# Copying the first pair's high rows by VectorE in a fused attention and MLP kernel

## The chip, the cores and the metric

The kernel runs on one core of a Trainium2 chip. A core has a matrix engine (TensorE, PE in the profile), a vector engine (VectorE, DVE), an activation engine (ScalarE, ACT), GpSimd (POOL) and a queue engine (SyncE, SP) that here only issues DMAs. The metric is the device time of one execution in microseconds (us), the median of three runs.

## The reference, cut to what matters

There are 4 batches, 8 heads, 576 tokens and a head width of 64. Attention with a decay comes first, then a gated MLP that also mixes tokens, then a second MLP with a gate. All of it is wanted in float32 accuracy.

```python
scores = scale * np.matmul(q, k.transpose(0, 1, 3, 2))
log_f = np.log(np.clip(f, 0.0001, 1.0))
cum = np.cumsum(log_f, axis=-1)
decay = cum[:, :, :, None] - cum[:, :, None, :]
scores = np.where(causal, -1000000000.0, scores + decay)
attn = softmax(scores)                     # written out in the reference
x = np.matmul(attn, v)                     # heads side by side: 512 wide
h = np.maximum(x @ w_in, 0.0)              # 512 -> 1024, halves u and v
v_n = (v - mean) / np.sqrt(var + 1e-06)
v_s = np.einsum('ts,bsd->btd', w_spatial, v_n) + b_spatial[None, :, None]
x = (u * v_s) @ w_out
xk = mu_k * x + (1.0 - mu_k) * x_prev      # the same with mu_r for xr
out = sigmoid(xr @ w_r) * (np.maximum(xk @ w_k, 0.0) ** 2 @ w_v)
```

## The kernel before

**Pairs of heads.** The 32 heads (batch by batch) are worked on as 16 pairs, numbered 0 to 15. For each pair q and k are loaded (`load`, L214), scaled by a power of two, and split into a high part in float16 (`qkhi`: `nq` by DVE on L258, `nk` by ACT on L256 for pair 0 and by POOL on L254 for the others) and the rest (`qklo`, L266 on DVE). Both parts lie side by side in `nk` and `nq`, and a DMA transpose (L268) turns them into the stacks `kT` and `qT` with 128 rows: 64 of one part, 64 of the other.

**The second stack.** A score is high times high plus the two cross products. `kT` times `qT` gives the cross products. The product of the high parts, with the decay, comes from a second pair of stacks: `kA` holds the 64 high rows of k and three rows of decay, `qA` the 64 high rows of q and three rows of a constant. The high rows are in `kT` and `qT` already and are copied from there: `kaux` (L274) copies rows 0 to 63 of `kT` to `kA`, `qaux` (L280) copies rows 64 to 127 of `qT` to rows 0 to 63 of `qA`. A copy is 64 rows of 1280 float16 values. L275 fetches the decay rows from DRAM (`cumd`). All four transfers are DMAs of the SP queue. The stacks exist three times: pair p uses stack p modulo 3.

**Scores, twice.** First the scores are made with queries as rows (`score`, L298: one matmul of `kT` and `qT`, then one of `kA` and `qA` into the same bank), DVE takes the row maxima from them (`rowmax`, L309), POOL scales these (L318), and ACT sums the exponentials (`rowsum`, L321). `mrow` puts maximum and logarithm of the sum into one row per query, turns it over by a matmul (L337), copies it (`mr`, L339 on DVE), and three small DMAs (L341) write it into three more rows of `qA`. Then the scores are made again with keys as rows (`scoreT`, L352), exponentiated (L362), cut to the causal part (L366 on POOL) and multiplied with v (L393).

**The MLPs.** The first MLP of a batch (L530 and L528, L598, L615) runs on PE between the attention of later pairs. The second MLP (L927) follows after the last pair. Weights arrive as 64-bit values and are converted by ACT and DVE (L103, L106, L110, L111).

**What sets the order.** Each step of each pair has a due time from the table `P` (two units for each pair), `run` emits the steps in order of due time, and a scheduler with its own model of time then fixes one order for each engine's instructions and for the DMAs of each queue. Steps under `high_priority(PRIO)` are preferred by it. `vl2` is the due time of the loads of v for batch 2 (L217). Every engine, and the SP queue, works strictly in its order: a DMA whose source isn't ready holds all DMAs behind it.

Of the kernel before, what the change touches and what calls it, by code (L numbers as in the profile page):

```python
# [25 lines left out]
T3 = ((0, 0), (0, 1), (1, 0))  # L26
# [3 lines left out]
SU = (((4, 0, 512, 0),), ((3, 0, 448, 0), (4, 512, 64, 448)), ((2, 0, 320, 0), (1, 0, 192, 320)), ((0, 0, 64, 0),))  # L30


P = dict(load=-8.0, sq=-5.52, ss=-5.2, sc=-5.0, hik=-5.196, lok=-4.166, hiq=-4.2, loq=-3.95, aux=-3.539, s=-2.53, m=-0.78, t=0.0, tu=0.426, th=0.412, pv0=0.2, pv1=0.9, out=1.405, rc=1.219, nr=1.831, xs=0.977, xl=1.55, rs=0.06, w1=-3.8, w0=2.0, s1=1.5, s0=6.8, wd=0.6, sd=0.6, wsp=9.493, eb=13.318, ed=1.1, crow=-4.2, mlp0=2.7, mlp1=2.7, mlp2=3.608, mlp3=2.7, len0=6.684, len1=6.952, len2=6.757, len3=4.319, T1=0.0, T2=0.0, T3=0.02, T4=0.0, T5=0.0, T6=0.0, T7=0.044, L1=0.0, L2=-0.017, L3=0.0, L4=0.0, L5=-0.224, L6=-0.408, L7=0.04, v0=-3.174, vs0=0.15, T8=0.0, T9=0.0, T10=0.0, T11=0.0, T12=-0.061, T13=-0.031, T14=0.069, T15=0.0, L0=0.0, L8=0.0, L9=0.0, L10=0.0, L11=0.0, L12=0.0, L13=-0.003, L14=0.0, L15=-0.24, vl1=-5.062, vq1=-2.7, vl2=-4.971, vq2=-2.898, vl3=-3.679, vq3=-3.376, lv0=0.238, lu0=0.381, lg0=0.249, lv1=0.238, lu1=0.381, lg1=0.199, lv2=0.238, lu2=0.381, lg2=0.436, lv3=0.346, lu3=0.381, lg3=0.701, n1=0.385, n2=0.508, n3=1.019, n4=1.161, gs=0.05, ta=3.45, tb=1.65, tc=0.22, fnb=1, fnk=1, fvn=1, fwf=0, fwin=0, fwsp=0)

PRIO = 300


def f32(ap):  # L40
# [3 lines left out]
class K:  # L44
# [201 lines left out]
    def qkhi(self, p, nm, eng):  # L246
# [5 lines left out]
        if eng == "act":  # L252
            if P["fnk"] > 0.5 and p >= 1:
                self.nc.gpsimd.tensor_scalar(hi, src, s, None, op0=ALU.mult)  # L254
# [15 lines left out]
    def kaux(self, p):  # L270

        nc = self.nc
        t = self.T["kA", p % 3]
        nc.sync.dma_start(t[0:64, 0:10], self.T["kT", p % 3][0:64, 0:10])  # L274
        nc.sync.dma_start(t[64:67, 0:10].rearrange("p (h c) t -> p h (c t)", h=2)[:, :, 64:640], self.cumd[:, 2 * p:2 * p + 2])  # L275

    def qaux(self, p):

        nc = self.nc
        nc.sync.dma_start(self.T["qA", p % 3][0:64], self.T["qT", p % 3][64:128])  # L280

    def crow(self, p):

# [28 lines left out]
    def rowsum(self, g, blocks):  # L312
# [4 lines left out]
        nb = self.at.tile([128, 10], F32, tag="nb", bufs=4, name="nb")  # L317
        (self.nc.gpsimd if P["fnb"] > 0.5 else self.nc.vector).tensor_scalar(nb[:, c], self.nm[p % 2][:, c], qa[:, 5:6], -1.0, op0=ALU.mult, op1=ALU.mult)  # L318
        for ib in blocks:
# [54 lines left out]
    def products(self, p, part):  # L374

        self.last = None
        with self.tc.high_priority(PRIO):
            if part == 0:
# [48 lines left out]
    def wconv(self, i):  # L427
# [3 lines left out]
        wf = self.wf[i] = self.stp.tile([128, 512], F32, tag="wf", bufs=4, name="wf")  # L431
        self.raw_convert(self.wst[i], wf, True, P["fwf"] > 0.5)
        self.sumsq(self.am[:, kc:kc + 1], wf, self.win[:, 0, kc, cs])
# [6 lines left out]
    def wsplit(self, i):  # L440
# [4 lines left out]
        hi, lo = self.win[:, 0, kc, cs], self.win[:, 1, kc, cs]  # L445
        self.pin(nc.gpsimd.tensor_scalar(hi, wf, s, None, op0=ALU.mult) if P["fwin"] > 0.5 else nc.scalar.mul(hi, wf, s))
        nc.vector.scalar_tensor_tensor(lo, wf, s, hi, ALU.mult, ALU.subtract)

    def weights_spatial(self):
# [300 lines left out]
    def early_norms(self):  # L750
# [127 lines left out]
    def m3(self, i):  # L878
# [265 lines left out]
```

## Time and profile before

| | |
|---|---|
| median of 3 runs | 689.62 us (688.99 to 691.65) |
| the profiled execution | 684.6 us, span of the core's work 682.9 us |
| PE busy | 616.9 us (90%) |
| DVE busy | 436.3 us (64%) |
| ACT busy | 462.7 us (68%) |
| POOL busy | 186.5 us (27%) |
| DMA | 69.74 MB |

A line of the profile gives the busy time of an engine or a group of instructions. Shares are averages over stages: attention with the first MLP takes about the first 350 us, the second MLP from about 420 us on is PE alone. [...]

### The profile page before, as it was taken

Reading aid. Unit: us, or ns where it says so; the run is one execution under the profiler, and the core shown is the slowest. Engines: PE = TensorE matmul, PEld = TensorE weight load, DVE = VectorE, ACT = ScalarE, POOL = GpSimd, SP = SyncE. Lnnn points to the kernel's source line nnn. Section 1 sums busy time; section 2 is a strip of 40 time slices with the busy share of each in tenths; the row PEclk is TensorE's granted clock in tenths of the full one; section 3 lists DMA queues with packets and bytes.
Section 4 is the critical chain, followed back from the end, with each engine's and each line's share of the span. In section 5 each row is a group of like instructions: output and inputs, shape, how many; then the busy total and the mean of one; then the engine's idle time right before and its main releaser. Section 6 shows DMA issues by size and latency. Waiting matters only on the chain.

```text
span 682.9 us, 11117 instructions
## 1 busy us (share of the span) xinstructions
PE 616.9 (90%) x3720; PEld 369.7 (54%) x3720; DVE 436.3 (64%) x1238; ACT 462.7 (68%) x1023; POOL 186.5 (27%) x420
## 2 busy tenths in 40 slices
PE   0478676998999999989999899999999999999997
PEld 0133333566545666446657544566655556566585
DVE  6885957879487867676137888997228524532342
ACT  4689899898879879788339599974328334442531
POOL 6342444674447743465106010000000000000000
PEclk9998898999999999999999999999999999999999
DMA  7984542627654555341046672313001100100010
GB/s 254 266 229 94 139 116 52 207 57 196 167 129 108 94 172 132 74 91 33 19 154 212 206 253 70 123 62 108 15 1 32 62 1 0 62 1 0 1 62 31
DMA packets 69343, 69.74 MB, mean 102 GB/s; under 512 B 46659, under 2 KB 47395, under 8 KB 69286
## 3 DMA queue, kind: packets, MB, share of 16 engines
q1 hardware_dynamic: 68854, 67.85, 35.5%
q10 hardware_dynamic: 432, 1.18, 0.4%
q8 instruction: 29, 0.48, 0.3%
q14 instruction: 28, 0.23, 0.1%
HBM read 43.61 MB, written 9.55 MB: 78 GB/s over the span
## 4 chain that ended last, share of the span: by engine, by line
PE 59%; DVE 14%; DMA 10%; ACT 7%; SPq 3%; issue 3%; POOL 2%; DVEq 0%; ACTq 0%
PE m L927 37%; PE o L393 4%; PE t L352 4%; DVE sx L309 4%; PE m L615 4%; PE s L298 3%; PE m1u L598 3%; DMA qA<-qT 3%; PE m1v L530 3%; SPq L341 2%; DMA qT<-nq 2%; ACT junk L70 2%; DMA wst<-in_moe_w_r_dram 2%; ACT junka L321 1%; DMA kT<-nk 1%
## 5 line engine op out<-in xcount | busy, mean ns | idle before, releaser
L321 ACT ACTIVATE junka<-sx,nb,qa 128x576 bf16<-128x576 f32 (+4 forms) x160 | 103.8, 648 | 20.5 <-POOL nb L318 17.3
L927 PE MATMUL m<-moe_w_v,k 128*128 128x512 f32 x432 | 111.6, 406 | 0.0
L927 PE MATMUL m<-xx,moe_w_k 128*128 128x512 f16 (+1 forms) x480 | 99.1, 358 | 0.6 <-ACT tmp L976 0.6
L927 PEld LDWEIGHTS m<-moe_w_v,k 128*128 128x128 f32 x432 | 80.7, 188 | 19.4
L309 DVE CUSTOM_DVE_ANT_0 sx<-s,mask 128x512 f32<-128x512 f32 (+4 forms) x160 | 72.5, 473 | 21.5 <-PE s L298 17.6
L298 PE MATMUL s<-kT,qT 128*128 128x512 f16 (+2 forms) x192 | 55.3, 308 | 25.3 <-DVE nm L309 14.2
L362 ACT ACTIVATE e<-t,qa 128x512 f32<-128x512 f32 x96 | 64.1, 680 | 18.5 <-PE t L352 18.0
L366 POOL TENSOR_SCALAR_AFFINE_SELECT e<-e 128x128 f32<-128x128 f32 x128 | 48.1, 388 | 85.2 <-ACT e L362 82.5
L927 PEld LDWEIGHTS <-moe_w_k 128*128 128x128 f16 x480 | 45.5, 98 | 47.6 <-issue 5.3
L976 ACT ACTIVATE tmp<-m,sx 128x512 f32<-128x512 f32 (+1 forms) x40 | 25.9, 647 | 58.6 <-PE m L927 58.6
L977 DVE TENSOR_TENSOR tmp<-tmp 128x512 f32<-128x512 f32 (+1 forms) x40 | 25.5, 638 | 56.9 <-ACT tmp L976 56.9
L393 PE MATMUL o<-e,v 128*64 128x64 f32 (+4 forms) x384 | 55.0, 410 | 5.2 <-DVE mr L339 1.9
L298 PE MATMUL s<-kA,qA 67*128 67x512 f16 (+2 forms) x192 | 49.0, 307 | 9.1 <-DMA qA<-qT 5.8
L899 POOL COPY x<-x 128x1 f32<-128x1 f32 x16 | 4.8, 313 | 185.5 <-ACT x L897 175.7
L615 PE MATMUL m<-wspT,vn 128*128 128x288 f16 x384 | 55.2, 286 | 0.2
L927 PE MATMUL m<-gh,moe_w_out 128*128 128x512 f16 (+1 forms) x240 | 50.9, 367 | 3.3 <-DVE gs L803 3.3
L352 PE MATMUL t<-qA,kA 70*128 70x512 f16 (+2 forms) x192 | 48.9, 292 | 3.9 <-DMA qA<-mr 2.9
L598 PE MATMUL m1u<-xt,win 128*128 128x288 f16 x384 | 52.3, 287 | 0.0
L352 PE MATMUL t<-qT,kT 128*128 128x512 f16 (+2 forms) x192 | 50.8, 292 | 0.0
L530 PE MATMUL m1v<-win,xt 128*128 128x512 f16 x192 | 49.4, 392 | 0.6 <-ACT xt L396 0.6
L927 PE MATMUL m<-moe_w_r,xx 128*128 128x512 f16 x216 | 48.0, 379 | 0.0
L949 DVE SCALAR_TENSOR_TENSOR mt<-x,mu,mt 128x64 f32<-128x64 f32 (+4 forms) x64 | 30.2, 514 | 26.7 <-ACT mt L947 26.7
(219 smaller groups left out, 1134.7 us busy)
## 6 DMA issues: line engine op xcount, KB each, us to landing
knat<-in_k_dram SPq DMA_DIRECT2D x16, 320.0 KB
v<-in_v_dram SPq DMA_DIRECT2D x20, 256.0 KB
gd<-u SPq DMA_DIRECT2D x16, 288.0 KB
gl<-gd SPq DMA_DIRECT2D x8, 576.0 KB
out_dram<-o SPq DMA_DIRECT2D x18, 256.0 KB
qnat<-in_q_dram SPq DMA_DIRECT2D x14, 320.0 KB
wst<-in_moe_w_k_dram SPq DMA_DIRECT2D x8, 512.0 KB
g<-gd SPq DMA_DIRECT2D x16, 256.0 KB
```

The costliest lines, as they stand in the source:

```text
L298: self.nc.tensor.matmul(s[:, o:o + n], self.tok(qn, p, h, 128 * ib - 64, 128)[0:r], self.tok(kn, p, h, k0, n)[0:r], start=(j == 0), stop=( ...
L309: self.nc.vector.tensor_tensor_reduce(out=self.sx[g][r0:, SO[ib] + k0:SO[ib] + k0 + n], in0=self.s[u % 2][r0:, o:o + n], in1=self.mask[r0: ...
L321: self.nc.scalar.activation(self.junka[r, 0:n], self.sx[g][r, SO[ib]:SO[ib] + n], AF.Exp, scale=qa[r, 5:6], bias=nb[r, i:i + 1], accum_out ...
L352: self.nc.tensor.matmul(t[:, o:o + n], self.tok(kn, p, h, 128 * c, 128)[0:r], self.tok(qn, p, h, q0, n)[0:r], start=(j == 0), stop=(j == 1))
L362: self.nc.scalar.activation(self.e[g][:, 512 * u:512 * u + 512], t, AF.Exp, scale=self.qa[p][:, 5:6])
L366: self.nc.gpsimd.affine_select(out=e, in_=e, pattern=[[1, 128]], compare_op=ALU.is_ge, fill=0.0, base=0, channel_multiplier=-1)
L393: self.chain(self.nc.tensor.matmul(o[r, 448 + f:448 + q1], v[:, c, pr, r], e, start=(c == 0), stop=(c == 4 or q1 == 64)))
L530: nc.tensor.matmul(self.m1p, xt[:, xs, 128 * j:128 * j + 128], self.win[:, ws, kc, 512:1024], **flags)
L598: self.nc.tensor.matmul(o, self.win[:, ws, kc, fs], self.xt[(4 * b + kc) % 8][:, xs, ts_], start=(kc == 0 and n == 0), stop=(kc == 3 and n ...
L615: nc.tensor.matmul(o, pairs[n][0], pairs[n][1], start=(n == 0), stop=(n == 13))
L927: self.nc.tensor.matmul(out, l, r, start=(first and j == 0), stop=(last and j == len(pairs) - 1))
L949: nc.vector.scalar_tensor_tensor(tmp[:, r0:r1], x2[:, kc, r0:r1], self.mu[:, w, 1, kc:kc + 1], tmp[:, r0:r1], ALU.mult, ALU.add)
```

## The change

For pairs below `NC`, which is 1, thus for pair 0 alone, the two copies of high rows are made by VectorE under the scheduler's preference. All other pairs keep their DMAs. In the table `P` one number differs: `vl2` is -3.989 where it was -4.971, so the five loads of v for batch 2 are due about half a pair's time later.

```diff
-P = dict(... vl2=-4.971, ...)
+P = dict(... vl2=-3.989, ...)
...
+NC = 1
...
         t = self.T["kA", p % 3]
-        nc.sync.dma_start(t[0:64, 0:10], self.T["kT", p % 3][0:64, 0:10])
+        if p < NC:
+            with self.tc.high_priority(PRIO):
+                nc.vector.tensor_copy(t[0:64, 0:10], self.T["kT", p % 3][0:64, 0:10])
+        else:
+            nc.sync.dma_start(t[0:64, 0:10], self.T["kT", p % 3][0:64, 0:10])
         nc.sync.dma_start(t[64:67, 0:10].rearrange("p (h c) t -> p h (c t)", h=2)[:, :, 64:640], self.cumd[:, 2 * p:2 * p + 2])
...
-        nc.sync.dma_start(self.T["qA", p % 3][0:64], self.T["qT", p % 3][64:128])
+        if p < NC:
+            with self.tc.high_priority(PRIO):
+                nc.vector.tensor_copy(self.T["qA", p % 3][0:64], self.T["qT", p % 3][64:128])
+        else:
+            nc.sync.dma_start(self.T["qA", p % 3][0:64], self.T["qT", p % 3][64:128])
```

Lines behind the edits have other numbers in the changed kernel (L268 is L269 there, L274 is L279, L275 is L280, L280 is L289, L341 is L350, L309 is L318). The scheduler gives new orders on all engines, from the first pair to the end. Three places matter below. In the names, kT_127, kA_128, qT_129 and qA_130 are the stacks of pairs 0, 3, 6 and so on, 131 to 134 those of pairs 1, 4, 7, and 135 to 138 those of pairs 2, 5, 8.

**VectorE at the start**, before: `qnat_89` and `knat_86` are pair 1's q and k, the L309 rows are pair 0's first row maxima.

```order
L258 TENSOR_SCALAR nq<-qnat_89,qa 128x10x64
L266 SCALAR_TENSOR_TENSOR nq<-qnat_89,qa,nq 128x10x64
L110 SCALAR_TENSOR_TENSOR wf<-wf,wst 128x512
L111 SCALAR_TENSOR_TENSOR wf<-wst,wf 128x512
L266 SCALAR_TENSOR_TENSOR nk<-knat_86,qa,nk 128x10x64
L309 ISA sx,nm_159<-s,mask 128x512
```

and in the changed kernel:

```order
L287 COPY qA_130<-qT_129 64x1280
L259 TENSOR_SCALAR nq<-qnat_89,qa 128x10x64
L267 SCALAR_TENSOR_TENSOR nq<-qnat_89,qa,nq 128x10x64
L111 SCALAR_TENSOR_TENSOR wf<-wf,wst 128x512
L277 COPY kA_128<-kT_127 64x1280
L112 SCALAR_TENSOR_TENSOR wf<-wst,wf 128x512
L318 ISA sx,nm_159<-s,mask 128x512
L318 ISA nm_159 128x1
L267 SCALAR_TENSOR_TENSOR nk<-knat_86,qa,nk 128x10x64
```

Both copies stand in front of the first row maximum, and pair 1's `nk` has moved behind it.

**The SP queue at the start**, from pair 0's decay rows to pair 1's last copy, before:

```order
L275 DMA kA_128<-cumd 3x2x576
L280 DMA qA_130<-qT_129 64x1280
L274 DMA kA_128<-kT_127 64x1280
L96 DMA wst<-in_moe_w_in_dram 128x1024
L217 DMA v_139<-in_v_dram 128x512 x5
L268 DMA_TRANSPOSE kT_131<-nk 128x10x128
L214 DMA knat_85<-in_k_dram 128x640
L268 DMA_TRANSPOSE qT_133<-nq 128x10x128
L214 DMA qnat_88<-in_q_dram 128x640
L274 DMA kA_132<-kT_131 64x1280
L275 DMA kA_132<-cumd 3x2x576
L280 DMA qA_134<-qT_133 64x1280
```

and in the changed kernel:

```order
L280 DMA kA_128<-cumd 3x2x576
L97 DMA wst<-in_moe_w_in_dram 128x1024
L218 DMA v_139<-in_v_dram 128x512 x5
L215 DMA knat_85<-in_k_dram 128x640
L269 DMA_TRANSPOSE qT_133<-nq 128x10x128
L269 DMA_TRANSPOSE kT_131<-nk 128x10x128
L215 DMA qnat_88<-in_q_dram 128x640
L280 DMA kA_132<-cumd 3x2x576
L289 DMA qA_134<-qT_133 64x1280
L279 DMA kA_132<-kT_131 64x1280
```

The two copies are gone from it, the loads behind them move up, and pair 1's q is transposed ahead of its k.

**The SP queue where `mr` rows and transposes meet.** Pair 5 (stacks 135 to 138), with the rows of pair 3 (qA_130<-mr), before:

```order
L275 DMA kA_136<-cumd 3x2x576
L268 DMA_TRANSPOSE qT_137<-nq 128x10x128
L341 DMA qA_130<-mr 1x10x128 x3
L268 DMA_TRANSPOSE kT_135<-nk 128x10x128
L280 DMA qA_138<-qT_137 64x1280
L214 DMA knat_87<-in_k_dram 128x640
L274 DMA kA_136<-kT_135 64x1280
```

and in the changed kernel:

```order
L280 DMA kA_136<-cumd 3x2x576
L269 DMA_TRANSPOSE qT_137<-nq 128x10x128
L269 DMA_TRANSPOSE kT_135<-nk 128x10x128
L350 DMA qA_130<-mr 1x10x128 x3
L279 DMA kA_136<-kT_135 64x1280
L289 DMA qA_138<-qT_137 64x1280
```

Pair 5's k is transposed ahead of pair 3's rows, no longer behind them.

Pair 7 (stacks 131 to 134) and pair 8 (135 to 138), with the rows of pair 5 (qA_138<-mr) and pair 6 (qA_130<-mr), before:

```order
L268 DMA_TRANSPOSE kT_131<-nk 128x10x128
L341 DMA qA_138<-mr 1x10x128 x3
L268 DMA_TRANSPOSE qT_133<-nq 128x10x128
L274 DMA kA_132<-kT_131 64x1280
L280 DMA qA_134<-qT_133 64x1280
...
L268 DMA_TRANSPOSE qT_137<-nq 128x10x128
L268 DMA_TRANSPOSE kT_135<-nk 128x10x128
L275 DMA kA_136<-cumd 3x2x576
L280 DMA qA_138<-qT_137 64x1280
L274 DMA kA_136<-kT_135 64x1280
...
L341 DMA qA_130<-mr 1x10x128 x3
```

and in the changed kernel:

```order
L350 DMA qA_138<-mr 1x10x128 x3
L280 DMA kA_132<-cumd 3x2x576
L269 DMA_TRANSPOSE kT_131<-nk 128x10x128
L269 DMA_TRANSPOSE qT_133<-nq 128x10x128
...
L269 DMA_TRANSPOSE qT_137<-nq 128x10x128
L218 DMA v_139<-in_v_dram 128x512
L215 DMA qnat_90<-in_q_dram 128x640
L289 DMA qA_138<-qT_137 64x1280
L218 DMA v_139<-in_v_dram 128x512
L350 DMA qA_130<-mr 1x10x128 x3
L269 DMA_TRANSPOSE kT_135<-nk 128x10x128
```

Here it is the other way round: pair 7's k and q both come behind pair 5's rows, and pair 8's k, which was ahead of pair 6's rows, comes behind them. Pair 11 has pair 7's exchange too: k, rows of pair 9, q before; rows of pair 9, k, q in the changed kernel. On PE, 10 matmuls of the first MLP's last product (L615) stand ahead of pair 8's first scores before, and 49 in the changed kernel. On ACT the squares of pair 2's q (L70) move one instruction ahead, in front of a weight's squares.

## Rows read from the trace of the kernel before

**Rows 1.** Busy time by stretches of 20 us; columns: engines, granted clock, DMA share, GB/s.
```profile
20.00:40.00 20.00, 10.73 (x43) 5.27 (x44) 16.73 (x57) 13.42 (x35) 7.34 (x10) 1.00 1.01 291
60.00:80.00 20.00, 13.44 (x69) 6.10 (x68) 15.59 (x47) 16.11 (x38) 8.42 (x14) 0.76 0.82 185
100.00:120.00 20.00, 14.53 (x91) 7.36 (x89) 15.26 (x57) 18.80 (x45) 8.63 (x18) 0.86 0.34 76
440.00:682.90 242.90, 239.03 (x1154) 146.27 (x1152) 115.12 (x238) 106.42 (x179) 1.47 (x8) 1.00 0.09 33
```

**Rows 2.** Chain of work that ended last; columns: start us, us, what.
```profile
25.49 4.55 DMA qT<-nq
30.06 4.23 DMA qA<-qT
...
98.01 3.48 DMA kT<-nk
101.50 2.68 DMA kA<-kT
```

**Rows 3.** Timeline of the SP queue, 10 to 60 us; columns: start us, us, instruction.
```profile
16.56 0.56 SPq L280 DMA_DIRECT2D qA<-qT  x1
...
23.14 1.56 SPq L268 DMA_TRANSPOSE kT<-nk  x1
...
28.03 0.47 SPq L274 DMA_DIRECT2D kA<-kT  x1
```

**Rows 4.** DMA issues by line: KB each.
```profile
qA<-qT SPq DMA_DIRECT2D x16, 160.0 KB
```

**Rows 5.** Timeline of VectorE, 16 to 23 us.
```profile
18.04 0.55 DVE L258 TENSOR_SCALAR nq<-qnat,qa 128x640 f16<-128x640 f32 x1
18.62 1.30 DVE L266 SCALAR_TENSOR_TENSOR nq<-qnat,qa,nq 128x640 f16<-128x640 f32 x1
...
20.56 1.76 DVE L111 SCALAR_TENSOR_TENSOR wf<-wst,wf 128x512 int32<-128x512 int32 x1
22.24 0.87 DVE L266 SCALAR_TENSOR_TENSOR nk<-knat,qa,nk 128x640 f16<-128x640 f32 x1
23.04 0.68 DVE L309 CUSTOM_DVE_ANT_0 sx<-s,mask 128x512 f32<-128x512 f32 x1
```

**Rows 6.** Timeline of all engines, 29 to 40 us; in brackets the idle time before.
```profile
29.98 0.61 ACT L70 ACTIVATE win<-wf 128x512 f16<-128x512 f32 x1
...
32.74 1.88 POOL L254 TENSOR_SCALAR nk<-knat,qa 128x640 f16<-128x640 f32 x1 [2.00 <-DVE qa L87]
32.76 1.11 DVE L258 TENSOR_SCALAR nq<-qnat,qa 128x640 f16<-128x640 f32 x1
...
35.12 0.69 DVE L309 CUSTOM_DVE_ANT_0 sx<-s,mask 128x512 f32<-128x512 f32 x1 [0.32 <-PE s L298]
```

**Rows 7.** Timeline around pair 5, VectorE: its k is split.
```profile
93.55 0.94 DVE L266 SCALAR_TENSOR_TENSOR nk<-knat,qa,nk 128x640 f16<-128x640 f32 x1
```

**Rows 8.** Timeline of the SP queue, 92 to 108 us: pair 5, rows of pair 3.
```profile
94.24 1.29 SPq L268 DMA_TRANSPOSE qT<-nq  x1
95.62 2.27 SPq L341 DMA_DIRECT2D qA<-mr  x3
```

**Rows 9.** Timeline of PE, 94 to 107 us: pair 5's first scores of the high parts.
```profile
104.22 0.56 PE L298 MATMUL s<-kA,qA 67*128 67x512 f16 x2 [1.68 <-DMA kA<-kT]
```

**Rows 10.** Timeline of the SP queue: pair 7's k.
```profile
131.78 1.36 SPq L268 DMA_TRANSPOSE kT<-nk  x1
```

**Rows 11.** Timeline of the SP queue: pair 11's k.
```profile
214.08 1.36 SPq L268 DMA_TRANSPOSE kT<-nk  x1
```

**Rows 12.** Timeline of the SP queue: pair 8's k, and the rows of pair 6.
```profile
155.36 1.34 SPq L268 DMA_TRANSPOSE kT<-nk  x1
...
162.63 2.36 SPq L341 DMA_DIRECT2D qA<-mr  x3
```

**Rows 13.** Chain of work, 160 to 350 us: the first MLP's last product.
```profile
179.01 2.70 PE m L615 x22
```

More of the change, by code (lines that the diff above doesn't have):

```diff
@@ L30 @@
 SU = (((4, 0, 512, 0),), ((3, 0, 448, 0), (4, 512, 64, 448)), ((2, 0, 320, 0), (1, 0, 192, 320)), ((0, 0, 64, 0),))
-P = dict(load=-8.0, sq=-5.52, ss=-5.2, sc=-5.0, hik=-5.196, lok=-4.166, hiq=-4.2, loq=-3.95, aux=-3.539, s=-2.53, m=-0.78, t=0.0, tu=0.426, th=0.412, pv0=0.2, pv1=0.9, out=1.405, rc=1.219, nr=1.831, xs=0.977, xl=1.55, rs=0.06, w1=-3.8, w0=2.0, s1=1.5, s0=6.8, wd=0.6, sd=0.6, wsp=9.493, eb=13.318, ed=1.1, crow=-4.2, mlp0=2.7, mlp1=2.7, mlp2=3.608, mlp3=2.7, len0=6.684, len1=6.952, len2=6.757, len3=4.319, T1=0.0, T2=0.0, T3=0.02, T4=0.0, T5=0.0, T6=0.0, T7=0.044, L1=0.0, L2=-0.017, L3=0.0, L4=0.0, L5=-0.224, L6=-0.408, L7=0.04, v0=-3.174, vs0=0.15, T8=0.0, T9=0.0, T10=0.0, T11=0.0, T12=-0.061, T13=-0.031, T14=0.069, T15=0.0, L0=0.0, L8=0.0, L9=0.0, L10=0.0, L11=0.0, L12=0.0, L13=-0.003, L14=0.0, L15=-0.24, vl1=-5.062, vq1=-2.7, vl2=-4.971, vq2=-2.898, vl3=-3.679, vq3=-3.376, lv0=0.238, lu0=0.381, lg0=0.249, lv1=0.238, lu1=0.381, lg1=0.199, lv2=0.238, lu2=0.381, lg2=0.436, lv3=0.346, lu3=0.381, lg3=0.701, n1=0.385, n2=0.508, n3=1.019, n4=1.161, gs=0.05, ta=3.45, tb=1.65, tc=0.22, fnb=1, fnk=1, fvn=1, fwf=0, fwin=0, fwsp=0)
+P = dict(load=-8.0, sq=-5.52, ss=-5.2, sc=-5.0, hik=-5.196, lok=-4.166, hiq=-4.2, loq=-3.95, aux=-3.539, s=-2.53, m=-0.78, t=0.0, tu=0.426, th=0.412, pv0=0.2, pv1=0.9, out=1.405, rc=1.219, nr=1.831, xs=0.977, xl=1.55, rs=0.06, w1=-3.8, w0=2.0, s1=1.5, s0=6.8, wd=0.6, sd=0.6, wsp=9.493, eb=13.318, ed=1.1, crow=-4.2, mlp0=2.7, mlp1=2.7, mlp2=3.608, mlp3=2.7, len0=6.684, len1=6.952, len2=6.757, len3=4.319, T1=0.0, T2=0.0, T3=0.02, T4=0.0, T5=0.0, T6=0.0, T7=0.044, L1=0.0, L2=-0.017, L3=0.0, L4=0.0, L5=-0.224, L6=-0.408, L7=0.04, v0=-3.174, vs0=0.15, T8=0.0, T9=0.0, T10=0.0, T11=0.0, T12=-0.061, T13=-0.031, T14=0.069, T15=0.0, L0=0.0, L8=0.0, L9=0.0, L10=0.0, L11=0.0, L12=0.0, L13=-0.003, L14=0.0, L15=-0.24, vl1=-5.062, vq1=-2.7, vl2=-3.989, vq2=-2.898, vl3=-3.679, vq3=-3.376, lv0=0.238, lu0=0.381, lg0=0.249, lv1=0.238, lu1=0.381, lg1=0.199, lv2=0.238, lu2=0.381, lg2=0.436, lv3=0.346, lu3=0.381, lg3=0.701, n1=0.385, n2=0.508, n3=1.019, n4=1.161, gs=0.05, ta=3.45, tb=1.65, tc=0.22, fnb=1, fnk=1, fvn=1, fwf=0, fwin=0, fwsp=0)
 PRIO = 300
+NC = 1
 def f32(ap):
```

## Prediction

> **What bounds the kernel now.** I read the busy times by stretches first. From 440 us to the end PE is busy 239.03 of 242.90 us at full clock [rows 1]; its order there is the same in both kernels, so nothing of the change can be won or lost in that stretch. The early stretches differ: between 60 and 80 us PE is busy 13.44 of 20 us at a granted clock of 0.76, between 100 and 120 us 14.53 at 0.86, with ACT at 18.80 of 20. Between 20 and 40 us the DMA engines are full (share 1.01, 291 GB/s). So what can move is the attention's first part, and there PE waits for something else.
>
> The chain of waits, read second, says for what: for a pair's stacks. Pair 1's way is a transpose of 4.55 us from 25.49 and a copy of high rows of 4.23 us from 30.06; pair 5's is 3.48 us from 98.01 and 2.68 us from 101.50 [rows 2]. Third I read the timelines of VectorE and of the SP queue where the orders differ. A row is followed by the next instruction only when that row is through, so an instruction put ahead costs all behind it.
>
> The profiled execution is 684.6 us (span 682.9, and 1.7 around it). The median of the runs is 689.62, 5.0 above. I work on the first and carry the difference to the second.
>
> **What the change removes and adds for pair 0.** It removes two DMAs of 160 KB [rows 4], 328 KB together; at 291 GB/s [rows 1] that is 1.1 us of a full DMA system. It adds two copies of 64 x 1280 float16 on VectorE. No row has such a copy. The nearest is the scaling of 128 x 640 float32 into float16, 0.55 us [rows 5]: with twice the columns 1.1 us a copy, which I take. The bounds are 0 below, and above it 2.3: twice the 0.87 us of the subtraction with two sources [rows 5], and 0.56 by which the same scaling took longer later, 1.11 us [rows 6].
>
> [...]
>
> **Step 1, the start.** Before, the first row maximum of pair 0 starts at 23.04 us, right behind pair 1's `nk` of 0.87 us at 22.24 [rows 5]. From 18.04 on one VectorE instruction follows on the other (in the one gap of these rows, at 19.9, the order has L110), so cover for the copies is nil: both stand inside this row, and `nk` goes behind the maximum. The maximum starts at 22.24 + 2 x 1.1 = 24.4, which is 1.4 later: for pair 0 the change is a loss, since the DMAs did the copies beside VectorE. `nk` then ends at 24.4 + 0.68 + 0.87 = 26.0. Its transpose was issued at 23.14 [rows 3] and is now issued at 26.0. Against that, q's transpose is no longer behind k's, and is early. Before, the last operand of pair 1 landed at 30.06 + 4.23 = 34.29 [rows 2]. Now it is k's: 26.0 + 4.55 + 4.23 = 34.8 with q's durations (k's own transpose took from 23.14 to 28.03, 4.89 [rows 3], much the same). That is +0.5, and the 1.1 us of DMA taken away make it -0.6. Bounds: with copies at 0, `nk` ends at 23.8, 2.2 earlier, so -2.8; with 2.3 each it is 2.4 later and nothing of the DMA time is won, so +2.9 (0.5 + 2.4).
>
> How much of a gain arrives is limited by what is late next. VectorE takes pair 1's maxima at 35.12 after an idle time of only 0.32 us, behind pair 2's split [rows 6]; and pair 2's squares pass a weight's 0.61 us on ACT [rows 6]. So of any gain here at most 0.32 + 0.61 = 0.9 us arrives unless those move too. I take -0.6.
>
> **Step 2, pair 5.** Its `nk` is ready at 93.55 + 0.94 = 94.49 [rows 7], but its transpose stood behind pair 3's three small DMAs, which hold the queue from 95.62 for 2.27 us [rows 8], and came out at 98.01 [rows 2]. Now it comes first, about 95.6: 2.4 earlier. The copy `kA` is then behind the small DMAs, which start when the transpose's issue of about 1.36 us (a like one [rows 10]) is through, at 97.0, and end at 99.3; it was issued at 101.50 [rows 2], so 2.2 earlier. PE waited 1.68 us for just this copy [rows 9]. But ACT is nearly full there [rows 1], and pair 3's rows are 1.4 later, which pushes its second scores. I take half of the 1.68: -0.8. Bounds -2.2 and +1.4.
>
> **Step 3, pairs 7 and 11.** Here the queue is changed the other way: k's transpose (1.36 us in both [rows 10, 11]) now stands behind the rows of two pairs earlier and so directly ahead of q's. For pair 7 the decay's DMA stands there too, about 0.47 us by a single issue [rows 3], so q's comes 1.8 later, for pair 11 1.4. Other work of PE can hide it. As in step 2 I take about half or less: +0.7 for pair 7, where attention is still the bound, and +0.5 for pair 11. Bounds 0 to 1.8 and 0 to 1.4.
>
> **Step 4, `vl2` and pair 8.** The five loads of v move among the preparations of pairs 7 and 8, and pair 8's k goes behind pair 6's rows. It was issued at 155.36; the rows come at 162.63 and take 2.36 [rows 12], so at 165.0 it is 9.6 later, if the rows come no earlier. The cover is the matmuls that PE now does first, 49 in place of 10: 39 x 2.70 / 22 = 4.8 us [rows 13]. The preparation is some pair ahead of its use, so I take nothing; the bound is what isn't covered, 9.6 - 4.8 = 4.8.
>
> **Sum:** -0.6 - 0.8 + 0.7 + 0.5 = -0.2 us, thus 684.4 for an execution like the profiled one, and 689.4 on the median's scale. All other new places in the order I cost at nothing, because they are exchanges of neighbours that both stay early.
>
> **Rivals.**
>
> A, faster. The copies cost almost nothing, the start gives its 0.9 us and pair 5 its full 2.2, and the exchanges of step 3 are hidden. PE's shorter waits also spare it low clock: 13.44 us busy at 0.76 would be 13.44 x 0.24 = 3.2 us shorter at full clock [rows 1]; half of it is 1.6. Sum -4.7, 684.9. For it speaks that the chain runs through both places [rows 2]; against it that VectorE has no gap at the start [rows 5] and ACT none around pair 5 [rows 1].
>
> B, slower. Transposes queued behind the small DMAs of an earlier pair set PE's waits: those rows come only after that pair's sums, so the preparation of the next pairs hangs on the end of the earlier. Place: pairs 7, 11, above all 8. It decides from where pair 8's delay exceeds its 4.8 us of cover. With half of the bound, +1.8 + 1.4 + 2.4, and the gains -0.6 - 0.8 kept, it is +4.2: 693.8. For it speaks that pair 5 before paid in just this way [rows 8, 9]; against it the preparation's lead and the matmuls moved ahead.
>
> C, the copies lock with POOL. The mechanism: a copy would wait for a whole POOL operation, like the 1.88 us of pair 2's `nk` [rows 6]; one such wait puts the first maximum and pair 1 back 1.9: 691.3. The same rows speak against it: VectorE's split at 32.76 starts 0.02 after that POOL operation and ends at 33.87, before POOL's end at 34.62; it was slowed to 1.11, not stopped. [...]
>
> That the change does nothing, because pair 2's way over ACT sets the time of the start and later pairs are early anyway, lies within the forecast: 689.6.
>
> **Chances.** Forecast 0.36, A 0.33, B 0.23, C 0.08. With three runs and a spread of the runs of 2.7 us, a change of about 0.5%, 3.4 us, can be told from none. A lies beyond it, B too; the forecast and C don't. So faster 0.33, same 0.44, slower 0.23. The likeliest case's own range is 686.5 to 692.5: below, pair 5's 2.2 and the start's 0.9 taken in full; above, the start's +2.9. The whole range goes from 681.4 (-2.8, -2.2 and all 3.2 of the clock) to 696.2: B with all 4.8 of pair 8, 1.8 and 1.4, less the gains of 1.4.
>
> **What the profile after would show.** The two copies on VectorE: near 1.1 us step 1 stands, near 0.5 its size is wrong by 1.2, near 2 C or the upper bound holds. First row maximum of pair 0 at about 24.4, not 23.04; pair 1's last copy landing near 34.8 (33.7 with lighter DMAs), not 34.29. PE's wait of 1.68 us for pair 5's `kA` smaller or gone. For pair 7 and 11 a wait for `qT` before their first scores of up to 1.8 us. For pair 8 its k's transpose issued well behind 155, and a wait of PE before its first scores if B is right. The granted clock in 60 to 80 us above 0.76 speaks for A. The forecast is wrong if PE starts the second MLP more than 3.4 us earlier or later than before; the stretch from there to the end must last as long as before, or the cause lies where I put none.

## The result, and the profile after

The changed kernel took 693.88 us (median of 9 runs, 692.13 to 695.28); the kernel before, on the same chip, 690.35 (688.83 to 692.26). The ratio is 1.0061, 95% interval 1.0037 to 1.0084: slower by 3.5 us (0.6%). The forecast was no change, 689.4, with 686.5 to 692.5 as its own range; the time came out above it, on the side of rival B. Executions far off the others of their kernel are left out of the ratios here and below, and as the profiled one of start_dma is among them (2164 us), that kernel has no profile to read.

The profiled execution of after is 694.96 us (span 693.2), a usual one. That of before, 684.6, lies below all of its nine runs. So the two profiles are 10.3 us apart where the kernels are 3.5 apart, and a difference between them isn't yet an effect of the change. Kernels below that keep the old order up to 140 us, with the copies as DMAs, show by how much that execution was early.

The busy times after, by stretches of 20 us (columns as in [rows 1]):

```profile
20.00:40.00 20.00, 9.88 (x39) 4.71 (x39) 17.41 (x57) 12.64 (x33) 7.60 (x9) 1.00 1.02 274
60.00:80.00 20.00, 11.88 (x73) 5.45 (x74) 15.80 (x53) 18.74 (x46) 9.45 (x15) 0.85 0.71 169
100.00:120.00 20.00, 16.73 (x93) 8.73 (x92) 15.24 (x59) 18.95 (x47) 9.29 (x18) 0.76 0.30 74
450.00:693.20 243.20, 239.53 (x1156) 146.58 (x1154) 115.08 (x238) 108.15 (x182) 1.47 (x8) 1.00 0.10 34
```

The last row answers to the last of [rows 1]: the second MLP lasts as long as before, 243 us, and only starts later. PE's first product of it (`xx` and `moe_w_k`) stands at 412.1 us before and at 423.0 after, and from there to the end it is 270.8 and 270.3 us. So the loss lies ahead of it. The clock is higher between 60 and 80 us (0.85, not 0.76) and lower between 100 and 120 (0.76, not 0.86), but this differs between executions of one order too: start_after and cut_200 below, with the same order up to 141 us, show 0.93 and 0.77 between 60 and 80. Two stretches that were not shown of before, first before:

```profile
140.00:200.00 60.00, 57.45 (x442) 36.31 (x440) 45.95 (x157) 51.13 (x122) 32.86 (x55) 1.00 0.54 137
200.00:260.00 60.00, 56.64 (x432) 35.22 (x430) 43.20 (x142) 52.57 (x132) 34.24 (x75) 0.97 0.54 128
```

and after:

```profile
140.00:200.00 60.00, 55.73 (x419) 35.52 (x417) 44.72 (x144) 49.47 (x118) 27.15 (x49) 0.97 0.46 112
200.00:260.00 60.00, 52.26 (x371) 31.11 (x369) 42.46 (x145) 47.86 (x123) 31.78 (x71) 0.91 0.47 120
```

PE does 442 + 432 instructions in these 120 us before and 419 + 371 after. It is idle 3.4 us of the second stretch before and 7.7 after, at a clock of 0.97 and 0.91. The waits of PE after, from the timeline (in brackets the idle time before):

```profile
189.71 0.39 PE L307 MATMUL s<-kA,qA 67*128 67x512 f16 x1 [1.18 <-DMA qA<-qT]
199.85 0.19 PE L307 MATMUL s<-kT,qT 128*128 128x64 f16 x1 [0.80 <-DVE nm L318]
202.13 0.23 PE L346 MATMUL o<-ident,nmh 128*128 128x128 f16 x1 [2.05 <-DVE ds L92]
202.82 1.33 PE L402 MATMUL o<-e,v 128*64 128x320 f32 x12 [0.46 <-DVE mr L348]
206.23 0.58 PE L361 MATMUL t<-qA,kA 70*128 70x512 f16 x1 [1.16 <-DMA qA<-mr]
```

They are steps of pairs 8 and 9 one behind the other: pair 9's copy of high rows, its last maxima, the turning of pair 8's rows (L346), the DMAs of these (`qA<-mr`), and at 206.23 pair 8's second scores. The waits add up to 5.65 us, and little else stands between these steps in PE's order. Before, PE's waits between 184 and 207 us are three, 1.32 us together:

```profile
191.47 0.30 PE L298 MATMUL s<-kT,qT 128*128 128x320 f16 x1 [0.25 <-DVE nm L309]
197.99 1.04 PE L530 MATMUL m1v<-win,xt 128*128 128x512 f16 x4 [0.32 <-ACT xt L396]
201.66 0.58 PE L298 MATMUL s<-kA,qA 67*128 67x512 f16 x2 [0.75 <-DMA qA<-qT]
```

The beginning of it after, on the SP queue:

```profile
155.07 1.38 SPq L269 DMA_TRANSPOSE qT<-nq  x1
160.75 2.36 SPq L350 DMA_DIRECT2D qA<-mr  x3
163.15 1.28 SPq L269 DMA_TRANSPOSE kT<-nk  x1
168.22 0.54 SPq L279 DMA_DIRECT2D kA<-kT  x1
```

and on PE:

```profile
168.16 1.02 PE L624 MATMUL m<-wspT,vn 128*128 128x288 f16 x7
169.01 0.57 PE L307 MATMUL s<-kT,qT 128*128 128x512 f16 x2
```

where before it was

```profile
157.97 1.39 PE L615 MATMUL m<-wspT,vn 128*128 128x288 f16 x10
159.20 0.38 PE L298 MATMUL s<-kT,qT 128*128 128x512 f16 x1
```

Pair 8's k is transposed at 163.15 (155.36 before [rows 12]), and its first scores start at 169.01 (159.20 before). The reader is to see that PE didn't wait for them: there is no bracket, and matmuls of the first MLP (L624, which is L615 before) stand right ahead. The order put the scores there. Behind them these matmuls are missing. (L615 is the first MLP's mixing over tokens, `w_spatial` times `v_n`. It is the last of its products that run between the pairs; the product with `w_out` follows later, in L927.)

### The profile page after: what moved, and what is told of

The parts are those of the page before. It is cut to its first block, busy times and chain, and to the rows that moved or that the text cites. A ratio compares the mean times of both kernels' runs of the same rounds, so it can differ in the third digit from the quotient of the medians.

```text
span 693.2 us, 11115 instructions
## 1 busy us (share of the span) xinstructions
PE 624.0 (90%) x3720; PEld 370.9 (53%) x3720; DVE 437.7 (63%) x1240; ACT 464.0 (67%) x1023; POOL 184.3 (27%) x420
## 4 chain that ended last, share of the span: by engine, by line
PE 59%; DVE 14%; ACT 9%; DMA 9%; issue 4%; POOL 2%; SPq 2%; DVEq 0%; ACTq 0%; POOLq 0%
PE m L936 37%; PE t L361 5%; PE m1v L539 4%; DVE sx L318 4%; PE o L402 4%; PE m L624 3%; PE s L307 3%; PE m1u L607 3%; ACT junka L330 3%; DMA wst<-in_moe_w_k_dram 2%; DMA qT<-nq 2%; DMA qA<-qT 1%; ACT junk L71 1%; SPq L350 1%; DMA kT<-nk 1%
## 5 line engine op out<-in xcount | busy, mean ns | idle before, releaser
L318 DVE CUSTOM_DVE_ANT_0 sx<-s,mask 128x512 f32<-128x512 f32 (+4 forms) x160 | 72.6, 473 | 22.1 <-PE s L307 19.5
L936 PEld LDWEIGHTS <-moe_w_k 128*128 128x128 f16 x480 | 45.5, 98 | 47.3 <-issue 5.0
L375 POOL TENSOR_SCALAR_AFFINE_SELECT e<-e 128x128 f32<-128x128 f32 x128 | 43.2, 350 | 97.4 <-ACT e L371 96.8
L307 PE MATMUL s<-kA,qA 67*128 67x512 f16 (+2 forms) x192 | 50.4, 309 | 8.8 <-DMA qA<-qT 4.5
L624 PE MATMUL m<-wspT,vn 128*128 128x288 f16 x384 | 56.9, 292 | 0.0
```

Of the source, the lines that this page charges most:

```text
L307: self.nc.tensor.matmul(s[:, o:o + n], self.tok(qn, p, h, 128 * ib - 64, 128)[0:r], self.tok(kn, p, h, k0, n)[0:r], start=(j == 0), stop=( ...
L318: self.nc.vector.tensor_tensor_reduce(out=self.sx[g][r0:, SO[ib] + k0:SO[ib] + k0 + n], in0=self.s[u % 2][r0:, o:o + n], in1=self.mask[r0: ...
L375: self.nc.gpsimd.affine_select(out=e, in_=e, pattern=[[1, 128]], compare_op=ALU.is_ge, fill=0.0, base=0, channel_multiplier=-1)
L624: nc.tensor.matmul(o, pairs[n][0], pairs[n][1], start=(n == 0), stop=(n == 13))
L936: self.nc.tensor.matmul(out, l, r, start=(first and j == 0), stop=(last and j == len(pairs) - 1))
```

## The experiments

To move one stretch of the order alone, a function at the end of the program ties each instruction of an engine to the one that is to stand ahead of it; a table `ORDER` gives the rows. Data dependences and waits stay as they are.

```diff
+def fixed(tc, nc):
+    rows = json.loads(zlib.decompress(base64.b64decode(ORDER)))
...
+    for e, row in rows.items():
+        last = None
+        for n in row:
+            i = made[e][n]
+            if last is not None:
+                tc.add_manual_dep(i, last.name, mybir.DependencyInfo(mybir.DependencyClass.NoSync, mybir.DependencyReason.DATA), reason="order")
+            last = i
...
         body(tc, args, out)
+        fixed(tc, nc)
```

Times given as stretches are those of the profiles. Ratios are to the kernel before, run on the same chip. The kernels of the table are explained one by one below it. The starts of a pair's second scores in the profiles (its first matmul of `scoreT` on `kT` and `qT`) show where time is lost, in us:

| kernel | pair 6 | pair 8 | pair 9 | pair 10 | pair 15 | ratio, interval |
|---|---|---|---|---|---|---|
| before (profiled) | 166.83 | 199.66 | 221.73 | 242.38 | 333.86 | 1 |
| copies_alone | 170.85 | 203.77 | 224.73 | 246.00 | 337.14 | 1.0020, 0.9994 to 1.0047 |
| before_w8 | 171.05 | 213.88 | 233.64 | 255.39 | 349.71 | 1.0141, 1.0102 to 1.0180 |
| late_200 | 171.10 | 204.01 | 224.82 | 252.18 | 342.78 | 1.0087, 1.0056 to 1.0118 |
| after | 165.79 | 206.60 | 224.23 | 251.54 | 342.16 | 1.0061, 1.0037 to 1.0084 |
| order_alone | 167.28 | 208.62 | 226.32 | 253.70 | 344.31 | 1.0092, 1.0057 to 1.0126 |
| after_w8 | 168.51 | 201.43 | 221.41 | 248.69 | 339.34 | 1.0046, 1.0020 to 1.0072 |
| start_after | 167.61 | 200.49 | 222.60 | 243.47 | 335.31 | 0.9976, 0.9954 to 0.9998 |
| cut_200 | 165.17 | 207.38 | 227.14 | 249.15 | 340.98 | 1.0032, 1.0008 to 1.0056 |
| k8_split | 166.90 | 209.02 | 229.16 | 251.11 | 344.92 | 1.0069, 1.0044 to 1.0093 |
| plan_only | 169.31 | 204.16 | 227.39 | 249.42 | 340.76 | 1.0020, 0.9996 to 1.0045 |
| copy_only | 164.22 | 205.45 | 222.29 | 249.97 | 345.10 | 1.0120, 1.0082 to 1.0159 |

The second to fourth kernels have the old order up to 140 us. All three reach pair 6 at 171, four us behind the execution that the prediction was worked out on. Those with the changed start, after to k8_split, reach it at 165 to 168.5. From pair 6 to pair 8 it is 32.8 to 32.9 us in the five that have the old order from 140 to 200 us, and 40.8 to 42.8 in the five that have the changed one (plan_only and copy_only have orders of their own, 34.9 and 41.2).

**Copies alone (copies_alone).** The table is the old order; the two copies stand on VectorE as after.

```diff
 DVE: L111 wf<-wst ...
+DVE: COPY qA<-qT ahead of pair 1's first nq, COPY kA<-kT between its L110 and L111
-SP:  L280 DMA qA_130<-qT_129, L274 DMA kA_128<-kT_127
```

> Pair 0's two copies on VectorE as in the changed kernel, every other instruction and DMA in the order of the kernel before. Theory W (the loss comes from the order between about 140 and 200 us, where pair 8's k is split and its scores made later): no difference, ratio 0.998 to 1.002. Rival C (the copies themselves cost, since pair 0's first scores of the high parts start at 23.23 us and not at 20.51, behind a copy that VectorE makes late): slower by 1 to 3 us, ratio 1.0015 to 1.0045. Rival L (the loss lies behind 200 us, in the order of pairs 10 to 15 and of the MLPs): no difference.

Ratio 1.0020 (0.9994 to 1.0047): no measurable cost. Rival C isn't excluded at its lower end, but it can't carry 3.5 us here, as the next kernel shows.

**The order alone (order_alone).** The table is the changed order; the two copies are DMAs of the SP queue behind pair 0's decay rows.

```diff
-DVE: COPY qA<-qT, COPY kA<-kT
+SP:  DMA qA_130<-qT_129, DMA kA_128<-kT_127, behind L280 kA_128<-cumd
```

> The changed kernel's order of everything, but pair 0's two copies are DMAs again, behind pair 0's decay rows as before. Theory W and rival L: the whole loss is still there, ratio 1.004 to 1.008. Rival C: the loss goes, ratio under 1.002.

Ratio 1.0092: the whole loss; that it is rather more is within the intervals. So the order costs, not the copies.

**The stretch from 140 to 200 us, put back in the changed kernel (after_w8).**

```diff
 SP, changed kernel with the old stretch:
-... qT_137<-nq, v, LOAD q, qA_138<-qT_137, v, qA_130<-mr x3, kT_135<-nk, v, ..., kA_136<-kT_135
+... qT_137<-nq, kT_135<-nk, kA_136<-cumd, qA_138<-qT_137, kA_136<-kT_135, ..., qA_130<-mr x3, v x3
 PE: 39 matmuls of L624 go behind pair 8's first scores; DVE, ACT and POOL likewise as before
```

> The changed kernel with one stretch of the order, about 140 to 200 us on all engines, as in the kernel before: pair 8's k is split ahead of pair 7's last maxima and transposed ahead of pair 6's small DMAs, and its scores come before most of the first MLP's last product. Theory W: the loss goes, ratio 0.997 to 1.002. Rivals C and L: it stays, ratio 1.004 to 1.008.

Ratio 1.0046: between the two. Pair 8 gets its 5 us back (201.43, not 206.60), but by pair 10 half is lost again. Theory W isn't all of it, and the change's rest costs something too.

**The same stretch of the changed order, in the kernel before (before_w8).**

```diff
 the same rows with + and - exchanged, in the kernel before
```

> The kernel before with only that stretch, about 140 to 200 us, in the changed kernel's order; the copies are DMAs. Theory W: the loss appears, ratio 1.004 to 1.009, and VectorE is idle some 7 us between 162 and 175 us as in the changed kernel. Rivals C and L: ratio under 1.002.

Ratio 1.0141: the stretch alone costs 9.7 us (0.0141 x 690) in the old kernel, more than the whole change and above theory W's range. VectorE's idle time is there as expected, 7.1 of 13 us, but from 167 to 180 us, as this execution reaches pair 6 some 5 us later than that of after. From pair 6's to pair 8's second scores its profile takes 213.88 - 171.05 = 42.8 us, where late_200, with the old order there, takes 32.9.

**Three cuts.** The order is the changed one up to a point and the old one behind: up to 141 us (start_after), up to 200 us (cut_200); and the other way round, old up to 200 us, changed behind, with DMAs (late_200).

```diff
 start_after: ORDER = changed[to 141 us] + old[rest]
 cut_200:     ORDER = changed[to 200 us] + old[rest]
 late_200:    ORDER = old[to 200 us] + changed[rest]
```

> The changed kernel's copies and order up to about 141 us (pair 7's first scores), everything behind that in the order of the kernel before. Theory W2 (the changed start and its order up to there gain 2 to 4 us, and all of the loss lies behind): ratio 0.994 to 0.999, the fastest version so far. Rival N (the two starts are equal, and what the single profiles show between them is scatter): 0.999 to 1.003, as the kernel with the copies alone.

> The changed kernel's order up to about 200 us, the rest in the order of the kernel before. Theory W (the stretch from 140 to 200 us is all of the loss): as the changed kernel, ratio 1.004 to 1.009. Rival L2 (a second loss of 3 to 5 us lies in the order of pairs 9 to 12, since the changed kernel stays at half of its loss when only the first stretch is put back): 1.000 to 1.004.

> The order of the kernel before up to about 200 us, copies by DMA, the rest in the changed kernel's order. Theory W: no difference, 0.998 to 1.002. Rival L2: slower by 3 to 5 us, 1.004 to 1.008, with waits of PE for the rows of pair 9 and for pair 12's transposes as in the changed kernel.

The changed start gains: 0.9976 (0.9954 to 0.9998), the lowest ratio of all, 1.7 us under before and about 6 under after. On top of it the stretch to 200 us costs 0.0056, 3.9 us (cut_200), and the rest then 0.0029, 2.0 us more (after), which the intervals alone don't tell from nothing. But after_w8 has the changed start and the changed rest without the stretch, and it lies 0.0070, 4.8 us, above start_after; there the stretch adds only 0.0015, 1.0 us. So with the changed start either part costs 4 to 5 us alone, and both cost 5.9 together. In the old order they cost 9.7 (before_w8) and 6.0 (late_200). Both W and L2 hold, each for a part, but the prices don't add: what a stretch costs depends on what stands around it.

The table shows where the rest costs: between pair 8's and pair 10's second scores it takes 48.2 us in late_200 and 47.3 in after_w8, but 42.2 in copies_alone and 43.0 in start_after, which have the old rest.

PE's part in the price of the stretch, start_after:

```profile
140.00:200.00 60.00, 56.71 (x437) 36.02 (x435) 46.58 (x160) 50.98 (x124) 31.41 (x51) 1.00 0.51 125
200.00:260.00 60.00, 56.03 (x424) 34.98 (x424) 43.55 (x144) 52.15 (x130) 34.40 (x75) 0.97 0.51 125
```

and cut_200:

```profile
140.00:200.00 60.00, 55.02 (x423) 34.98 (x421) 44.99 (x147) 50.03 (x120) 27.24 (x49) 1.00 0.48 112
200.00:260.00 60.00, 53.34 (x396) 31.99 (x396) 43.28 (x145) 49.34 (x125) 33.16 (x73) 0.97 0.51 126
```

PE is idle 1.7 + 2.7 = 4.4 us more, near the 3.9 of the times, at the same clock (the two profiled executions are 5.6 us apart); start_after has no wait over 1 us between 190 and 207 us, and cut_200 has again

```profile
200.03 0.19 PE L310 MATMUL s<-kT,qT 128*128 128x64 f16 x1 [0.81 <-DVE nm L321]
202.31 0.23 PE L349 MATMUL o<-ident,nmh 128*128 128x128 f16 x1 [2.06 <-DVE ds L95]
203.00 1.39 PE L405 MATMUL o<-e,v 128*64 128x320 f32 x12 [0.46 <-DVE mr L351]
```

**The due time alone (plan_only), and the copies with the old due time (copy_only).** Here the scheduler makes its own order.

```diff
 plan_only:  P = dict(... vl2=-3.989 ...), NC = 0
 copy_only:  P = dict(... vl2=-4.971 ...), NC = 1
```

> Only the due time of the loads of v for batch 2 is changed; copies by DMA; the scheduler makes its order anew, which leaves pair 8's k ahead of pair 6's small DMAs as before. Theory W: no difference, 0.997 to 1.003, so the new order around pair 8 comes from the two copies and not from the due time. Rival V (the later loads of v themselves cost): 1.004 or more.

> Only the two copies are changed; the due time of batch 2's loads of v is the old one, and the scheduler makes its order anew. Pair 8's k again comes behind pair 6's small DMAs, with four loads of v between them too. Theory F (the copies set off the new order, whose early use of the first MLP's matmuls is the loss, and the due time doesn't mend it): ratio 1.004 to 1.012. Rival V2 (the changed order is due to the due time): 0.998 to 1.002.

plan_only is 1.0020 (0.9996 to 1.0045) and keeps pair 8's k ahead; copy_only is 1.0120 (1.0082 to 1.0159), twice the loss of the whole change. So the two copies set off a new order at pair 8, though 130 us lie between, and with the due time changed too the loss is half as large. That half isn't at pair 8: by the table copy_only is ahead of after up to pair 10 (249.97, not 251.54) and 2.9 us behind it by pair 15. So theory F's ratio came, but pair 8's matmuls are not all of it.

**Does pair 8's k have to be earlier, or its scores (k8_split)?** In cut_200 only pair 8's k is moved up; PE's order is untouched.

```diff
 DVE: L318 sx<-s (pair 7's second maximum)
+DVE: L267 nk<-knat,qa,nk (pair 8)
...
-DVE: L267 nk<-knat,qa,nk (pair 8), behind pair 7's last maximum
 SP:  qT_137<-nq, v, LOAD q
+SP:  kT_135<-nk
 SP:  qA_138<-qT_137, v, qA_130<-mr x3
-SP:  kT_135<-nk, v, ...
+SP:  kA_136<-kT_135
```

> As the kernel that has the changed order up to 200 us and the old one behind (ratio 1.0032), but pair 8's k is split earlier on VectorE (behind pair 7's second maximum, at about 157.5 us and not at 161) and transposed and copied earlier on the SP queue; PE's order is left, with 39 more matmuls of the first MLP's last product ahead of pair 8's first scores. Theory F (those matmuls, used up early and missing behind pair 8, are the loss): no difference to that kernel, 1.001 to 1.006, and PE's first scores of pair 8 stay near 169 us though its stacks are ready some 5 us before. Rival S (the late split and transpose themselves are the wait): 0.996 to 1.001.

The queue in the profile:

```profile
159.20 1.35 SPq L272 DMA_TRANSPOSE kT<-nk  x1
162.00 2.35 SPq L353 DMA_DIRECT2D qA<-mr  x3
164.46 0.53 SPq L282 DMA_DIRECT2D kA<-kT  x1
```

and PE:

```profile
169.75 0.53 PE L627 MATMUL m<-wspT,vn 128*128 128x288 f16 x3
170.12 0.57 PE L310 MATMUL s<-kT,qT 128*128 128x512 f16 x2
```

In cut_200 the same rows are

```profile
163.89 1.28 SPq L272 DMA_TRANSPOSE kT<-nk  x1
168.51 0.54 SPq L282 DMA_DIRECT2D kA<-kT  x1
168.54 0.56 PE L310 MATMUL s<-kT,qT 128*128 128x512 f16 x2
172.93 0.56 PE L310 MATMUL s<-kA,qA 67*128 67x512 f16 x2 [0.59 <-DMA kA<-kT]
```

The transpose goes out 4.7 us before that of cut_200, the copy 4.0 us before, and the first scores stand at 170.12: nothing is gained. The only wait for pair 8's k in cut_200 is the 0.59 us at 172.93; it is gone in k8_split, and pair 8's second scores still start 42.1 us behind pair 6's (42.2 in cut_200). Rival S is out. The ratio, 1.0069, is not below cut_200's and lies above theory F's range too (its interval, from 1.0044, reaches into it). In the profile the clock is 0.91 between 160 and 180 us, where cut_200 has 1.00: 24 equal matmuls (L627) take 4.78 us there and 3.10 in cut_200. Without that the first scores would stand at about 168.4, as in cut_200. Whether the clock is so in all executions isn't shown. So it isn't a wait for pair 8's k that costs. What is left is the order on the engines, and on PE the matmuls stand right ahead of the scores; a kernel in which PE's order alone is moved was not run.

**The changed start with DMAs (start_dma).** As start_after, the two copies as DMAs at their old place.

```diff
-DVE: COPY qA<-qT, COPY kA<-kT
+SP:  DMA qA_130<-qT_129, DMA kA_128<-kT_127, behind L280 kA_128<-cumd
```

> As the kernel that has the changed start up to 141 us and the old order behind (ratio 0.9976), but pair 0's two copies are DMAs again, at their old place in the SP queue. Theory O (the gain of the changed start is in its order, pairs 3 to 6, and the copies matter little): 0.995 to 0.9995. Rival D (the gain comes from the two DMAs that are gone): 1.000 to 1.004.

Ratio 0.9987 (0.9962 to 1.0012). It lies in theory O's range, but its interval reaches into rival D's and holds start_after's 0.9976 too; how much of the start's gain is the order and how much the copies stays open.

**What PE's order shows.** The number of the first MLP's matmuls (L528, L530, L598, L615) that stand ahead of a place in PE's order:

| ahead of | before | after |
|---|---|---|
| pair 8's first scores | 178 | 217 |
| pair 9's first scores | 296 | 289 |
| pair 9's second scores | 364 | 328 |
| pair 10's second scores | 446 | 436 |

Between pair 8's first and pair 9's second scores there are 186 before and 111 after. Each of the two parts takes about half of that away: 147 are left in cut_200 (the stretch puts 39 ahead of pair 8's first scores) and 150 in after_w8 and late_200 (the rest puts 36 behind pair 9's second scores). There PE has these matmuls to do while maxima and exponentials of pairs 8 and 9 are made, and there the idle time stands: PE is idle for 3.2 us between the two places in start_after, 6.9 in cut_200, 5.1 and 5.3 in after_w8 and late_200, and 7.2 in after. That the missing matmuls are the cause is read from these counts and waits; no kernel moves them alone.

## Why the prediction was wrong

**Step 4 failed, and so did the sentence that put all other places at nothing.** Step 4 said of pair 8: "The cover is the matmuls that PE now does first, 49 in place of 10", and: "I take nothing". It took matmuls that are moved ahead for cover of a wait. They are work that PE does in any case, and by the counts above they are missing where PE is idle some 30 us later. The measured price of that stretch, of which pair 8 is the part that the step looked at, is 3.9 us with the changed start (cut_200 less start_after), 9.7 in the old kernel (before_w8) and about 1 where the rest is changed too, where I had 0 with a bound of 4.8. In k8_split pair 8's stacks were ready ahead of their use, and it didn't help. The other failed term is "All other new places in the order I cost at nothing": the order behind 200 us costs 4.8 us alone with the changed start (after_w8 less start_after), 6 in the old order (late_200) and 2.0 on top of the stretch. Both parts together cost 5.9 and the start gains 1.7, which leaves the 4.2 of the ratio, 1.0061.

**Rival B had the sign and one of the places.** That its 693.8 lies by the measured 693.88 is luck, since its mechanism isn't what is seen. It let transposes wait behind the small DMAs. Pair 8's came 7.8 us later, not 9.6, but in after the small DMAs held it only from 161.9, when its source was ready on VectorE (161.02 + 0.89), to 163.15; PE had no wait for it, and k8_split took the delay away and gained nothing. At pairs 7 and 11, where B saw 1.8 and 1.4, pair 7's exchange is part of start_after, which is faster than before, and pair 11's first scores have no wait in after. Which rows of the order behind 200 us cost isn't settled. In late_200 PE waits there for pair 9's rows (1.07 us) and pair 12's transposes (1.45) and runs at 0.91 from 200 to 260 us; pair 12's transposes are not behind small DMAs there, they go out as soon as VectorE has split their sources (k's at 244.89, its source at 243.99 + 0.88).

**Step 1 was near on the rows, partly by luck, and small in effect.** The copies and the first maximum after, on VectorE:

```profile
18.16 1.06 DVE L287 COPY qA<-qT 64x1280 f16<-64x1280 f16 x1
22.71 0.47 DVE L277 COPY kA<-kT 64x1280 f16<-64x1280 f16 x1
23.97 0.69 DVE L318 CUSTOM_DVE_ANT_0 sx<-s,mask 128x512 f32<-128x512 f32 x1 [0.19 <-PE s L307]
```

24.4 was forecast and 23.97 came; pair 1's k was issued at 25.50 (26.0 forecast). But 1.1 us a copy was not its price: the first took 1.06 beside an operation of POOL, the second 0.47. In cut_200 and others both take half a microsecond (0.49 and 0.48), and the maximum comes at 22.28, ahead of the 23.04 of before (last section). Pair 1's last copy had landed by 33.17, when PE takes its scores of the high parts without a wait (34.38 before); 34.8 was forecast. The 4.89 us that the step read for k's transpose end at the issue of a copy that stood behind other DMAs in the queue; after, it took at most 3.4 (25.50 to 28.93). Yet pair 1's first maximum comes at 35.99, not 35.12, since pair 2's split stands ahead of it on VectorE and starts at 34.04, not 32.76:

```profile
33.17 0.96 PE L307 MATMUL s<-kA,qA 67*128 67x512 f16 x2
35.99 0.68 DVE L318 CUSTOM_DVE_ANT_0 sx<-s,mask 128x512 f32<-128x512 f32 x1
```

So the -0.6 doesn't arrive there. That pair 0 loses by the change is seen on PE, which got its first scores of the high parts at 23.23 and not at 20.51. Nothing measurable of it reaches the end (copies_alone).

**Step 2 held on the queue.** Pair 5's k went out at 94.16 and its copy at 98.10 (forecast 95.6 and 99.3), and PE's first scores of the high parts have no wait ([rows 9] 1.68). About half of that wait came back ahead of it, for the transpose:

```profile
94.16 1.46 SPq L269 DMA_TRANSPOSE kT<-nk  x1
95.71 2.29 SPq L350 DMA_DIRECT2D qA<-mr  x3
98.10 0.53 SPq L279 DMA_DIRECT2D kA<-kT  x1
```

and on PE:

```profile
97.79 0.86 PE L307 MATMUL s<-kT,qT 128*128 128x512 f16 x2 [0.89 <-DMA kT<-nk]
102.75 1.01 PE L307 MATMUL s<-kA,qA 67*128 67x512 f16 x2
```

**Step 3** cost nothing that shows. Pair 7 has a wait of 0.63 us for `qA<-qT` after,

```profile
141.04 0.39 PE L307 MATMUL s<-kA,qA 67*128 67x512 f16 x1 [0.63 <-DMA qA<-qT]
```

but before it had one of 0.85 for the transpose at this place,

```profile
139.11 0.58 PE L298 MATMUL s<-kT,qT 128*128 128x512 f16 x2 [0.85 <-DMA qT<-nq]
```

and pair 11 has none. The order up to 141 us, which holds steps 1, 2 and pair 7's part of step 3 among other exchanges, gains 1.7 us in start_after (0.1 to 3.2 by its interval), where the sum had -0.6 - 0.8 + 0.7 = -0.7. How the gain divides among them isn't shown.

**Rival A** asked for a gain of 4.7 us; the whole changed start gains 1.7. Its sign, a clock above 0.76 between 60 and 80 us, came (0.85), but 100 to 120 us lost what was gained there, and among executions with this start that clock goes from 0.77 to 0.93. That shorter waits of PE spare it low clock was the author's assumption and isn't shown: between 60 and 80 us PE is idle 8.1 us after, at the higher clock, and 6.6 before. **Rival C** is answered below. **The scale** was a weak point, but not what failed: the sum was worked out on an execution 4 us early by pair 6. The waits that it read there are about the usual ones (pair 5's 1.68 us is 1.81 in late_200, pair 7's 0.85 is 0.86). What was unusual is the clock, 0.93 over the first 140 us, where copies_alone and late_200 have 0.90. That a difference of 5.0 to the median could simply be carried over was an assumption.

## What to carry to other kernels

Work that an in-order engine can do at any time is a store that others' waits can be filled from; the counts here agree with that, though it isn't shown by itself. A new order that spends it early, or puts it off, shows no wait at that place, so count, between two places of the order, how much of it is left, and not only what stands ahead of a late operand. When a scheduler makes the order, a small edit at the start can cost most where it is not: fix the order, move one stretch at a time, test the stretches in more than one setting, since their prices need not add, and keep the part that gains (here the changed start with the old rest). And set a profiled execution against several others of the same order before a difference of a few us is read from it, its granted clock first.

## What the runs showed of the hardware

The copy of 64 x 1280 float16 takes 0.47 to 0.49 us in eleven of fourteen records (two copies in each of seven kernels) and 1.02 to 1.06 in the other three, not the 1.1 that was taken from the float32 scaling. The first copy meets POOL's `nk` of pair 1, and two patterns occur. In after, copies_alone and start_after:

```profile
18.08 1.90 POOL L255 TENSOR_SCALAR nk<-knat,qa 128x640 f16<-128x640 f32 x1 [5.08 <-DMA kT<-nk]
```

with the copy at 1.02 to 1.06 us. In cut_200, after_w8, k8_split and copy_only:

```profile
18.11 2.22 POOL L258 TENSOR_SCALAR nk<-knat,qa 128x640 f16<-128x640 f32 x1 [5.11 <-DMA kT<-nk]
```

(2.24 in copy_only) with the copies and the first maximum on VectorE, of cut_200:

```profile
18.16 0.49 DVE L290 COPY qA<-qT 64x1280 f16<-64x1280 f16 x1
21.01 0.48 DVE L280 COPY kA<-kT 64x1280 f16<-64x1280 f16 x1
22.28 0.69 DVE L321 CUSTOM_DVE_ANT_0 sx<-s,mask 128x512 f32<-128x512 f32 x1 [0.19 <-PE s L310]
```

The same instructions, for these rows in the same order: either POOL takes 1.90 and VectorE's copy 1.06, or POOL 2.22 and the copy 0.49, and the first maximum is at 23.97 (24.46 in copies_alone) or at 22.28. POOL's operation starts first in both, by 0.05 to 0.12 us, so what decides between them isn't shown. The copy, begun second, ends first in all seven: at 19.22 in after, where POOL's operation lasts to 19.98, and at 18.65 in cut_200, where it lasts to 20.33. Rival C's wait for a whole POOL operation doesn't occur; a loss of 0.6 us on one copy does, in some executions, and with the two VectorE instructions behind the copy it comes to 1.7 us.

The granted clock stands in parts of full speed. In slices of 1 us between 60 and 80 us of before it is 0.50 in nine, 1.00 in nine, and 0.74 and 0.88 in the two others; the 0.76 of that stretch is their mean.
